# PSUM tiles of one bank from the beginning, and values and crosses of a double step taken pair of heads by pair of heads

## The chip, the core and the metric

The kernel runs on one core of one Trainium2 chip. The metric is the device time of one execution in microseconds. Three runs of the kernel before took 953.83, 954.51 and 955.61 us, so its median is 954.51 us. One further execution was profiled.

## The reference

A decayed linear attention (8 batches, 8 heads, 576 positions, head size 64) is followed by a feed-forward layer with a softplus, over all 4,608 tokens, in float32:

```python
scores = scale * np.matmul(q, k.transpose(0, 1, 3, 2))
Dmat = np.where(rel >= 0, gamma[:, None, None] ** rel[None, :, :], 0.0)
attn = np.matmul(scores * Dmat[None], v)                    # B, H, S, D
x = attn.transpose(0, 2, 1, 3).reshape(B * S, H * D)         # 4608 x 512
h = x @ w_in                                                 # 512 -> 2048
g = np.maximum(h, 0.0) + np.log1p(np.exp(-np.abs(h)))
out = g @ w_out                                              # 2048 -> 512
```

## The kernel before

**Attention.** The tokens are cut into 36 chunks of 128, and the heads into 4 pairs. The decays are moved into q, k and v by scale factors, so that a chunk of a pair of heads needs masked scores within the chunk, their product with v (the *values*), a product of q with a running state of 64 x 64 per head (the *crosses*), and a new state. A cross is left out in the first chunk of a batch, and where a batch starts at row 64 of a chunk it covers 64 columns.

The first 9 chunks are computed in plain float32, in 18 *double steps* `m` of two pairs of heads each (`s` is the pair, `h` the head in it). `scores_double` (L154) gives TensorE four score matmuls (L160, 64 rows of weights by 128 columns of weights) and four state matmuls (L165, weights of 128 rows by 64 columns). `scores_double_out` (L169) has VectorE read them out with the mask (L175) and read out the state (L184 or L186), and GpSimd decays the state (L188). `values_double` (L191) gives TensorE four value matmuls (L200, weights 128 rows by 64 columns) and then four crosses (L206, weights 64 rows by 64 columns), which add to what the value matmuls wrote. `values_double_out` (L210) has ScalarE (L215) and VectorE (L216) write the result as a high and a low part into the x tile. TensorE works a float32 matmul off in two passes, each with its own weight load, so every such matmul has two MATMUL rows in the trace. The other 27 chunks go one pair at a time through matmuls of rounded parts (L265, L274, L347); the change doesn't touch them.

**Feed-forward.** 9 units of 512 tokens times 16 pieces of the hidden layer give 144 *slots*. Slot `i` has 12 matmuls of 512 columns for the hidden piece (`hidden_mm`, L379), the logarithm and exponential on ScalarE (L387 to L389), the softplus and its split on VectorE and ScalarE (L393 to L398), and 12 matmuls of 512 columns for the output of the slot before (`output_mm`, L411).

**The order is written out by hand** and each engine works its instructions off in that order. The *opening* runs double steps 0 to 8 before the first slot, while inputs and the first weight pieces are still arriving: in turn `scores_double(m)` and `values_double(m - 1)`. Double step 8 ends in slot 0: its values come behind the 12 hidden matmuls. Then every odd slot begins with `scores_double` and every even one with `values_double`, for double steps 9 to 17, up to slot 18. All of this is on TensorE between the matmuls of the slots. SyncE issues the loads; a load into a buffer waits until that buffer has been read.

**PSUM** has 8 banks of 512 float32 columns. Before, the attention tiles hold two banks each. In the opening three of them (`ps_open`: two for the scores in turn, one for the values of every other step) lie in six banks on the right, and one (`ps_att`) in the two on the left. In front of slot 0 the pool on the right is closed, and its banks go to the hidden tiles (`ps_h`, two) and the output tiles (`ps_y`, four); their first users wait for the last readers of the closed pool. From slot 0 on, scores and values take the one tile on the left in turn, so `scores_double(9)` waits until L216 has read the values of step 8:

```python
idle = two_banks(3)                                        # L504
open_pools.close()                                         # L537
later["ps_h"] = ctx.enter_context(tc.tile_pool(name="ps_h", bufs=2, space=PSUM, side="right"))
scores_double(m, two_banks(2))                             # L549
```

Of the kernel before, what the change touches and what calls it, by code (L numbers as in the profile page):

```python
# [7 lines left out]
F32 = mybir.dt.float32  # L8
# [5 lines left out]
PSUM = bass.MemoryType.PSUM  # L14


B, H, S, D = 8, 8, 576, 64
DM, DF = 512, 2048
NTOK = B * S
P = 128  # L20
C = 128
# [3 lines left out]
T = 512  # L25
CPU = T // C
# [7 lines left out]
AHEAD = STEPS // 2 + 1  # L34
# [25 lines left out]
def retention_softplus_ffn(ctx: ExitStack, tc, opening, first, others, w, dec, vsc, gchp, out):  # L60
    nc = tc.nc
# [6 lines left out]

    nc.scalar.preload_act_table_set("natural_log_exp_and_others")


    open_pools, plain_pools, weight_pools = ExitStack(), ExitStack(), ExitStack()
    ps_open = open_pools.enter_context(tc.tile_pool(name="ps_open", bufs=1, space=PSUM, side="right"))
    ps_att = plain_pools.enter_context(tc.tile_pool(name="ps_att", bufs=1, space=PSUM))
    rawp = plain_pools.enter_context(tc.tile_pool(name="rawp", bufs=2))
    pconst = plain_pools.enter_context(tc.tile_pool(name="pconst", bufs=1))
    wst = weight_pools.enter_context(tc.tile_pool(name="wst", bufs=WBUFS, side="right"))
    later = {}
# [15 lines left out]
    live = {}  # L94
# [56 lines left out]
            for n in range(4):  # L151
                nc.scalar.activation(v[:, n], v[:, n], AF.Copy, scale=f[:, n:n + 1])

    def scores_double(m, bank):  # L154

        L = live[-1 - m]
        for s in range(2):
            for h in range(2):
                rows = slice(h * D, (h + 1) * D)
                nc.tensor.matmul(bank[:, h, s * C:(s + 1) * C], L["k"][rows, s], L["q"][rows, s], start=True, stop=True)  # L160
        if _chunk_kind(m // 2)[1]:
            for s in range(2):
                for h in range(2):
                    rows = slice(h * D, (h + 1) * D)
                    nc.tensor.matmul(bank[rows, 0, 2 * C + s * D:2 * C + (s + 1) * D], L["kp"][:, s, rows],  # L165
                                     L["v"][:, s, rows], start=True, stop=True, skip_group_check=True)
        L["bank"] = bank

    def scores_double_out(m):  # L169
        L = live[-1 - m]  # L170
        start, follows = _chunk_kind(m // 2)
        a = moe.tile([P, 2, 2, C], F32, tag="osb", name="a2")
        msk = mask2 if start else mask
        for h in range(2):
            nc.vector.tensor_mul(a[:, h], L["bank"][:, h, 0:2 * C].rearrange("p (s c) -> p s c", s=2),  # L175
                                 msk.unsqueeze(1).broadcast_to([P, 2, C]))
        L["a"] = a
        L["before"] = states.get(m % 2)
        states[m % 2] = None
        if follows:  # L180
            st = L["bank"][:, 0, 2 * C:3 * C].rearrange("p (s d) -> p s d", s=2)
            s = att.tile([P, 2, D], F32, tag="s", name="s2", bufs=NPAIR + 1)
            if start is None:
                nc.vector.tensor_add(s, st, L["before"])  # L184
            else:
                nc.vector.tensor_copy(s, st)  # L186
            half = m % 2
            nc.gpsimd.tensor_mul(s, s, gchp0_sb[:, 2 * half:2 * half + 2].unsqueeze(2).broadcast_to([P, 2, D]))  # L188
            states[m % 2] = s

    def values_double(m, bank):  # L191
        L = live[-1 - m]
        start, _ = _chunk_kind(m // 2)
        n_cross = C if start is None else start
        if L["before"] is None:
            n_cross = 0
        for s in range(2):
            for h in range(2):
                rows = slice(h * D, (h + 1) * D)
                nc.tensor.matmul(bank[rows, s, 0:C], L["v"][:, s, rows], L["a"][:, h, s], start=True,  # L200
                                 stop=not n_cross, skip_group_check=True)
        if n_cross:
            for s in range(2):
                for h in range(2):
                    rows = slice(h * D, (h + 1) * D)
                    nc.tensor.matmul(bank[rows, s, 0:n_cross], L["before"][rows, s], L["q"][rows, s, 0:n_cross],  # L206
                                     start=False, stop=True, skip_group_check=True)
        L["o"] = bank

    def values_double_out(m):  # L210
        o = live.pop(-1 - m)["o"][:, :, 0:C]
        ch, pr = m // 2, 2 * (m % 2)
        xt = x_tile(ch // CPU)
        cols = slice((ch % CPU) * C, (ch % CPU + 1) * C)
        nc.scalar.copy(xt[:, HI, pr:pr + 2, cols], o)  # L215
        nc.vector.tensor_sub(xt[:, LO, pr:pr + 2, cols], o, xt[:, HI, pr:pr + 2, cols].bitcast(F32))  # L216
# [152 lines left out]
    ys = {}  # L369

    def hidden_mm(i, cols=slice(0, T)):

        u, p = divmod(i, NF)
        xt = x_tile(u)
        h = later["ps_h"].tile([P, T], F32, tag="h", name="h")[:, cols]
        n = 0
        for a, b in TERMS:
            for kt in range(NKT):
                nc.tensor.matmul(h, ws[p][:, a, kt * P:(kt + 1) * P], xt[:, b, kt, cols],  # L379
                                 start=(n == 0), stop=(n == 3 * NKT - 1))  # L380
                n += 1
        return h
# [18 lines left out]
    def output_mm(i):  # L401
        u, p = divmod(i, NF)
        parts = gs.pop(i)
        if p == 0:
            ys[u] = [later["ps_y"].tile([P, DM], F32, tag=f"y{n}", name=f"y{n}") for n in range(CPU)]
        for tt in range(CPU):
            y = ys[u][tt]
            for n, (a, b) in enumerate(TERMS):
                g = parts[tt * len(parts) // CPU]
                at = tt % (CPU // len(parts)) * P  # L410
                nc.tensor.matmul(y, g[:, a, at:at + P], ws[p][:, b, PIECE:],  # L411
                                 start=(p == 0 and n == 0), stop=(p == NF - 1 and n == 2))
# [83 lines left out]
            load_double(next_double[0])  # L496
            next_double[0] += 1

    def two_banks(n):
        pool, tag = ((ps_open, "open0"), (ps_open, "open1"), (ps_att, "bank"), (ps_open, "open2"))[n]  # L500
        return pool.tile([P, 2, 4 * C], F32, tag=tag, name="bank")


    idle = two_banks(3)  # L504
    for n in range(OPENING):
        nc.tensor.matmul(idle[:, n % 2, 0:2 * C], fill[:, 0:P], fill[:, 0:2 * C], start=True, stop=True)
    scale_next()
    scale_next()
    scale_values(0)
    for m in range(AHEAD):  # L510
        if m < AHEAD - 1:
            scores_double(m, two_banks(m % 2))
        if m > 0:
            values_double(m - 1, two_banks(2 + m % 2))
        if m == AHEAD - 1:
            scores_double(m, two_banks(m % 2))
            values_double_out(m - 1)
        if m in (2, 3, 4, 7, 8):
            load_next()
        if m in (3, 5, 7):  # L520
            load_weight((m + 1) // 2)
        scale_values(m + 1)
        scores_double_out(m)
        if m in (2, 4, 7):
            weight_b(m // 2 - 1)
        if m in (3, 5):
            weight_d((m - 3) // 2)
        if 0 < m < AHEAD - 1:
            values_double_out(m - 1)
        if m in (2, 4, 7):  # L530
            weight_c(m // 2 - 1)
        if m in (1, 3, 6):
            weight_a(m // 3)
        scale_next()
    weight_d(START_WEIGHTS - 1)
    wpos[0] = START_WEIGHTS
    open_pools.close()  # L537
    later["ps_h"] = ctx.enter_context(tc.tile_pool(name="ps_h", bufs=2, space=PSUM, side="right"))
    later["ps_y"] = ctx.enter_context(tc.tile_pool(name="ps_y", bufs=1, space=PSUM, side="right"))


    SPLIT = NPLAIN - LEAD
    deferred = [lambda: None]
    for i in range(NSLOT):
        j = i + LEAD
        if i < SPLIT:
            m = AHEAD + (i - 1) // 2
            if i % 2:
                scores_double(m, two_banks(2))  # L549
                scores_double_out(m)  # L550
                scale_next()
                if "raw" in later:
                    load_upto(NPLAIN + 1)
            elif i:
                values_double(m, two_banks(2))
                values_double_out(m)
                load_next()
            weight_step()
# [16 lines left out]
                scale_step(j + 2)  # L575
        else:
            scores_mm(j)
            bank = later["ps_os"].tile([P, 4 * C], F32, tag="os", name="os")
            value_mm(j - 1, bank)
            state_mm(j, bank)  # L580
            scale_step(j + 2)
            rest = value_out(j - 1)
            scores_out(j)
# [7 lines left out]
            break  # L591
        h = hidden_mm(i)
        if i == 0:
            values_double(AHEAD - 1, two_banks(2))
        ab = logs(h)
        if i == 0:
            values_double_out(AHEAD - 1)
# [85 lines left out]
```

## Time and profile before

| | |
|---|---|
| median of three runs | 954.51 us (953.83 to 955.61) |
| time of the profiled execution | 954.67 us |
| its span, first to last instruction | 952.9 us |
| TensorE matmul busy | 942.0 us, 99% of the span |
| ScalarE, VectorE, GpSimd busy | 676.9, 665.2 and 279.7 us |
| mean granted TensorE clock | 1.000 of full speed |

The profiled execution lasts 1.8 us longer than its span, and 0.16 us longer than the median of the runs. The chain of waits names, going back from the last instruction, what each step waited for; it shows where time can be won or lost. Rows of a timeline give the start of a group, the time from its first start to its last end, and, in brackets, how long the engine stood idle before it. Matmuls are pipelined, so such a group reaches into the next one: how long it holds TensorE is the distance from its start to the start of the next group.

### The profile page before, as it was taken

Reading aid. Unit: us, or ns where it says so; the run is one execution under the profiler, and the core shown is the slowest. Engines: PE = TensorE matmul, PEld = TensorE weight load, DVE = VectorE, ACT = ScalarE, POOL = GpSimd, SP = SyncE. Lnnn points to the kernel's source line nnn. Section 1 sums busy time; section 2 is a strip of 40 time slices with the busy share of each in tenths; the row PEclk is TensorE's granted clock in tenths of the full one; section 3 lists DMA queues with packets and bytes.
Section 4 is the critical chain, followed back from the end, with each engine's and each line's share of the span. In section 5 each row is a group of like instructions: output and inputs, shape, how many; then the busy total and the mean of one; then the engine's idle time right before and its main releaser. Section 6 shows DMA issues by size and latency. Waiting matters only on the chain.

```text
span 952.9 us, 14502 instructions
## 1 busy us (share of the span) xinstructions
PE 942.0 (99%) x4946; PEld 789.4 (83%) x4946; DVE 665.2 (70%) x1507; ACT 676.9 (71%) x1449; POOL 279.7 (29%) x497
## 2 busy tenths in 40 slices
PE   8899999999999999999999999999999999999998
PEld 6677778888888888888888888888888888888886
DVE  6688855777877777777777777777777777753222
ACT  6677756777877777777777777777777777764444
POOL 5122103333342332333343333233333333310000
PEclk9999999999999999999999999999999999999999
DMA  8556623212312132212212132213212222201001
GB/s 299 199 171 205 199 82 112 59 58 67 98 63 67 52 109 67 64 53 94 80 55 67 58 104 67 67 51 111 67 50 67 67 95 67 67 1 45 1 1 44
DMA packets 28729, 79.85 MB, mean 84 GB/s; under 512 B 3440, under 2 KB 3440, under 8 KB 28656
## 3 DMA queue, kind: packets, MB, share of 16 engines
q1 hardware_dynamic: 28656, 78.93, 26.1%
q8 instruction: 39, 0.64, 0.3%
q14 instruction: 34, 0.28, 0.1%
HBM read 69.48 MB, written 9.44 MB: 83 GB/s over the span
## 4 chain that ended last, share of the span: by engine, by line
PE 96%; DMA 2%; SPq 0%; POOL 0%; issue 0%; ACT 0%; POOLq 0%
PE h L379 42%; PE y L411 41%; PE os L347 6%; PE sc L265 3%; PE os L274 2%; DMA raw_g<-first 1%; PE bank L160 1%; PE bank L200 1%; PE bank L206 1%; DMA raw_rawp<-first 1%; PE bank L165 0%; SPq L437 0%; SPq L120 0%; POOL raw_g L136 0%; SPq L110 0%
## 5 line engine op out<-in xcount | busy, mean ns | idle before, releaser
L379 PE MATMUL h<-xt,w 128*128 128x512 f32 (+1 forms) x1740 | 420.6, 390 | 1.3 <-DVE s L186 1.3
L411 PE MATMUL y<-w,g 128*128 128x512 f32 x1728 | 414.9, 389 | 0.0
L411 PEld LDWEIGHTS y<-w,g 128*128 128x128 f32 x1728 | 324.3, 188 | 67.2
L379 PEld LDWEIGHTS h<-xt,w 128*128 128x128 f32 x1740 | 316.8, 188 | 63.5 <-ACT wst L443 1.4
L240 POOL TENSOR_TENSOR raw<-raw,dec_sb 128x256 f32<-128x256 f32 x108 | 98.3, 910 | 436.7 <-DMA raw<-others 404.6
L398 DVE TENSOR_TENSOR g<-ab,g 128x512 fp32r<-128x512 f32 (+1 forms) x145 | 101.3, 699 | 96.6 <-ACT g L397 96.6
L397 ACT CAST g<-ab 128x512 fp32r<-128x512 f32 (+1 forms) x145 | 89.5, 617 | 109.0 <-DVE ab L393 107.8
L393 DVE SCALAR_TENSOR_TENSOR ab<-h,ab 128x512 f32<-128x512 f32 (+1 forms) x145 | 99.6, 687 | 84.8 <-ACT ab L389 82.2
L387 ACT ACTIVATE ab<-h 128x512 f32<-128x512 f32 (+1 forms) x145 | 86.3, 595 | 76.6 <-PE h L379 76.4
L389 ACT ACTIVATE ab<-ab 128x512 f32<-128x512 f32 (+1 forms) x145 | 91.3, 630 | 4.6
L388 ACT ACTIVATE ab<-ab 128x512 f32<-128x512 f32 (+1 forms) x145 | 91.2, 629 | 4.6
L254 ACT CAST hl<-raw 128x768 fp32r<-128x768 f32 x108 | 91.0, 842 | 0.7 <-POOL raw L245 0.7
L284 DVE TENSOR_TENSOR a<-sc,a 128x256 f32<-128x256 f32 x108 | 45.8, 424 | 61.9 <-ACT a L283 61.6
L360 ACT CAST xt<-os 64x128 fp32r<-64x128 f32 x216 | 56.3, 261 | 44.3 <-PE os L274 40.1
L256 DVE TENSOR_TENSOR hl<-raw,hl 128x512 fp32r<-128x512 f32 x108 | 85.2, 789 | 1.5
L347 PE MATMUL os<-ah,hl 128*128 128x256 f32 x324 | 72.7, 285 | 0.0
L364 DVE TENSOR_TENSOR xt<-os,xt 64x128 fp32r<-64x128 f32 x216 | 62.3, 288 | 2.8
L308 POOL TENSOR_TENSOR s<-s,gchp_sb 128x128 f32<-128x128 f32 x96 | 59.4, 619 | 10.6 <-DVE s L307 0.2
L347 PEld LDWEIGHTS os<-ah,hl 128*128 128x128 f32 x324 | 53.3, 191 | 0.1
L285 POOL TENSOR_SCALAR_AFFINE_SELECT a<-a 128x256 f32<-128x256 f32 x108 | 44.2, 409 | 28.4 <-DVE a L284 26.7
L255 DVE TENSOR_TENSOR hl<-raw,hl 64x256 fp32r<-64x256 f32 x108 | 45.9, 425 | 7.6 <-ACT hl L254 4.6
L316 ACT CAST ah<-a 128x256 fp32r<-128x256 f32 x108 | 44.0, 407 | 7.6 <-POOL a L285 4.6
(84 smaller groups left out, 784.9 us busy)
## 6 DMA issues: line engine op xcount, KB each, us to landing
raw<-others SPq DMA_DIRECT2D x108, 384.0 KB, 3.1
wst<-w SPq DMA_DIRECT2D x32, 512.0 KB, 3.9
out<-osb SPq DMA_DIRECT2D x34, 256.0 KB, 2.2
raw_rawp<-first SPq DMA_DIRECT2D x13, 512.0 KB, 4.6
raw_g<-first SPq DMA_DIRECT2D x3, 512.0 KB, 7.5
raw_ab<-first SPq DMA_DIRECT2D x2, 256.0 KB, 8.6
dec_sb<-dec SPq DMA_DIRECT2D x1, 512.0 KB, 3.8
out<-part SPq DMA_DIRECT2D x2, 256.0 KB, 2.8
```

Source lines behind the costliest of these rows:

```text
L240: nc.gpsimd.tensor_mul(r[:, 2:4], r[:, 2:4], later["dec"][:, 2 * pr:2 * pr + 2])
L254: nc.scalar.copy(hl[:, 0:6], r)
L256: nc.vector.tensor_sub(hl[:, 6:10], r[:, 2:6], hl[:, 2:6].bitcast(F32))
L347: nc.tensor.matmul(o[:, :, 0:width], lhs, rhs, start=(n == 0), stop=(n == len(mms) - 1))
L379: nc.tensor.matmul(h, ws[p][:, a, kt * P:(kt + 1) * P], xt[:, b, kt, cols], start=(n == 0), stop=(n == 3 * NKT - 1))
L387: nc.scalar.activation(ab, h, AF.Abs)
L388: nc.scalar.activation(ab, ab, AF.Exp, scale=-1.0)
L389: nc.scalar.activation(ab, ab, AF.Ln, bias=1.0)
L393: nc.vector.scalar_tensor_tensor(ab, h, 0.0, ab, op0=ALU.max, op1=ALU.add)
L397: nc.scalar.copy(g[:, HI], ab)
L398: nc.vector.tensor_sub(g[:, LO], ab, g[:, HI].bitcast(F32))
L411: nc.tensor.matmul(y, g[:, a, at:at + P], ws[p][:, b, PIECE:], start=(p == 0 and n == 0), stop=(p == NF - 1 and n == 2))
```

## The change

All PSUM tiles have one bank, and the pools of the later stage are there from the beginning: `ps_y` (four banks) and `ps_h` (two) on the right, `ps_att` with two single banks on the left. The scores of a double step of the opening take two of the output banks in turn (y0 and y1, or y2 and y3), its values one of the two banks on the left. No pool is closed before slot 0. From slot 0 on the scores take both banks on the left, one for each head, and the values one. The values of both pairs of heads stand now in the right half of one bank, and the matmuls that write them are taken in another order: values and crosses of the first pair of heads, then values and crosses of the second.

```diff
-    open_pools, plain_pools, weight_pools = ExitStack(), ExitStack(), ExitStack()
-    ps_open = open_pools.enter_context(tc.tile_pool(name="ps_open", bufs=1, space=PSUM, side="right"))
-    ps_att = plain_pools.enter_context(tc.tile_pool(name="ps_att", bufs=1, space=PSUM))
+    ps_y = ctx.enter_context(tc.tile_pool(name="ps_y", bufs=1, space=PSUM, side="right"))
+    ps_h = ctx.enter_context(tc.tile_pool(name="ps_h", bufs=2, space=PSUM, side="right"))
+    plain_pools, weight_pools = ExitStack(), ExitStack()
+    ps_att = plain_pools.enter_context(tc.tile_pool(name="ps_att", bufs=2, space=PSUM))
...
-    def scores_double(m, bank):
+    def scores_double(m, banks):
...
-                nc.tensor.matmul(bank[:, h, s * C:(s + 1) * C], L["k"][rows, s], L["q"][rows, s], start=True, stop=True)
+                nc.tensor.matmul(banks[h][:, s * C:(s + 1) * C], L["k"][rows, s], L["q"][rows, s], start=True, stop=True)
...
+        o = bank[:, 2 * C:4 * C].rearrange("p (s c) -> p s c", s=2)
         for s in range(2):
             for h in range(2):
                 rows = slice(h * D, (h + 1) * D)
-                nc.tensor.matmul(bank[rows, s, 0:C], L["v"][:, s, rows], L["a"][:, h, s], start=True,
+                nc.tensor.matmul(o[rows, s], L["v"][:, s, rows], L["a"][:, h, s], start=True,
                                  stop=not n_cross, skip_group_check=True)
-        if n_cross:
-            for s in range(2):
-                for h in range(2):
-                    rows = slice(h * D, (h + 1) * D)
-                    nc.tensor.matmul(bank[rows, s, 0:n_cross], L["before"][rows, s], L["q"][rows, s, 0:n_cross],
-                                     start=False, stop=True, skip_group_check=True)
-        L["o"] = bank
+            for h in range(2) if n_cross else ():
+                rows = slice(h * D, (h + 1) * D)
+                nc.tensor.matmul(o[rows, s, 0:n_cross], L["before"][rows, s], L["q"][rows, s, 0:n_cross],
+                                 start=False, stop=True, skip_group_check=True)
+        L["o"] = o
...
-    idle = two_banks(3)
+    def bank():
+        return ps_att.tile([P, 4 * C], F32, tag="bank", name="bank")
+    idle = ps_h.tile([P, T], F32, tag="h", name="idle")
...
     for m in range(AHEAD):
+        pair = [ps_y.tile([P, 4 * C], F32, tag=f"y{2 * (m % 2) + h}", name="pair") for h in range(2)]
         if m < AHEAD - 1:
-            scores_double(m, two_banks(m % 2))
+            scores_double(m, pair)
         if m > 0:
-            values_double(m - 1, two_banks(2 + m % 2))
+            values_double(m - 1, bank())
...
-    open_pools.close()
-    later["ps_h"] = ctx.enter_context(tc.tile_pool(name="ps_h", bufs=2, space=PSUM, side="right"))
-    later["ps_y"] = ctx.enter_context(tc.tile_pool(name="ps_y", bufs=1, space=PSUM, side="right"))
...
-                scores_double(m, two_banks(2))
+                scores_double(m, [bank() for _ in range(2)])
...
-                values_double(m, two_banks(2))
+                values_double(m, bank())
```

On VectorE, ScalarE, GpSimd and SyncE the instructions stand in the same order as before; only TensorE's order differs. In the rows below `a_...` is the masked scores, `s_...` the state, `raw_...` a loaded input of a double step, `h` and `y` the hidden and output tiles, `w_...` and `xt_...` the weights and the x tile.

TensorE at the end of the opening (double steps 6, 7 and 8), before:

```order
L200 MATMUL bank<-a_356,raw_rawp 64x128 x4
L206 MATMUL bank<-raw_rawp,s_292 64x128 x4
L200 MATMUL bank<-a_394,raw_rawp 64x128 x4
L206 MATMUL bank<-raw_rawp,s_327 64x128 x4
L160 MATMUL bank<-raw_g 128x128 x4
L165 MATMUL bank<-raw_g 64x64 x4
L379 MATMUL h<-xt_190,w_94 128x512 x12
```

and now, where L203, L207, L162, L167 and L380 are the lines that were L200, L206, L160, L165 and L379:

```order
L203 MATMUL bank<-a_366,raw_rawp 64x128 x2
L207 MATMUL bank<-raw_rawp,s_300 64x128 x2
L203 MATMUL bank<-a_366,raw_rawp 64x128 x2
L207 MATMUL bank<-raw_rawp,s_300 64x128 x2
L203 MATMUL bank<-a_405,raw_rawp 64x128 x2
L207 MATMUL bank<-raw_rawp,s_336 64x128 x2
L203 MATMUL bank<-a_405,raw_rawp 64x128 x2
L207 MATMUL bank<-raw_rawp,s_336 64x128 x2
L162 MATMUL pair<-raw_g 128x128 x4
L167 MATMUL pair<-raw_g 64x64 x4
L380 MATMUL h<-xt_195,w_97 128x512 x12
```

Groups of four have become groups of two, and values and crosses alternate twice as often; nothing else has moved.

TensorE in front of and behind the hidden matmuls of slot 0, with the semaphores that an instruction waits for, before:

```order
L379 MATMUL h<-xt_190,w_94 128x512 [waits DVE_49,PE_49,Activation_49]
L379 MATMUL h<-xt_190,w_94 128x512
L379 MATMUL h<-xt_190,w_94 128x512 [waits Activation_49]
L379 MATMUL h<-xt_190,w_94 128x512 x9
L200 MATMUL bank<-a_429,raw_g 64x128 x4
L206 MATMUL bank<-raw_g,s_359 64x64 x4
L160 MATMUL bank<-raw_rawp 128x128 [waits DMAHW7_49,DVE_49,Pool_49]
L160 MATMUL bank<-raw_rawp 128x128 x3
```

and now (from the seventh hidden matmul on, with the five behind it):

```order
L380 MATMUL h<-xt_195,w_97 128x512 [waits DVE_49]
L380 MATMUL h<-xt_195,w_97 128x512 x5
L203 MATMUL bank<-a_441,raw_g 64x128 [waits DVE_49] x2
L207 MATMUL bank<-raw_g,s_369 64x64 x2
L203 MATMUL bank<-a_441,raw_g 64x128 x2
L207 MATMUL bank<-raw_g,s_369 64x64 x2
L162 MATMUL bank<-raw_rawp 128x128 [waits DMAHW7_49,PE_49,Pool_49]
L162 MATMUL bank<-raw_rawp 128x128 [waits DVE_49]
L162 MATMUL bank<-raw_rawp 128x128 x2
```

The first hidden matmul no longer waits for VectorE: that wait stands now at the fifth and seventh, which read the low part of the x tile. The wait for VectorE in front of the scores of step 9 has gone from their first matmul to their second, which writes the bank of the values of step 8.

TensorE at the front of an even slot, before:

```order
L411 MATMUL y_543<-w_96,g 128x512 x3
L200 MATMUL bank<-a_625,raw_rawp 64x128 x4
L206 MATMUL bank<-raw_rawp,s_432 64x128 x4
L379 MATMUL h<-xt_190,w_98 128x512 x12
L411 MATMUL y_540<-w_97,g 128x512 x3
```

and now:

```order
L412 MATMUL y_549<-w_99,g 128x512 x3
L203 MATMUL bank<-a_632,raw_rawp 64x128 x2
L207 MATMUL bank<-raw_rawp,s_444 64x128 x2
L203 MATMUL bank<-a_632,raw_rawp 64x128 x2
L207 MATMUL bank<-raw_rawp,s_444 64x128 x2
L380 MATMUL h<-xt_195,w_101 128x512 x12
```

Between the 512-column matmuls stand the same eight small ones, with three changes between L203 and L207 where there was one.

## Rows read from the trace of the kernel before

**Rows 1.** Chain of waits that ended last, share of the span by line.

```profile
PE h L379 42%; PE y L411 41%; PE os L347 6%; PE sc L265 3%; PE os L274 2%; DMA raw_g<-first 1%; PE bank L160 1%; PE bank L200 1%; PE bank L206 1%; DMA raw_rawp<-first 1%; PE bank L165 0%; SPq L437 0%; SPq L120 0%; POOL raw_g L136 0%; SPq L110 0%
```

**Rows 2.** Busy time by stretch: the span's microseconds, their sum, then each engine.

```profile
32.00:152.00 120.00, 120.00 (x701) 93.43 (x702) 87.99 (x159) 82.63 (x141) 20.11 (x25) 1.00 0.51 165
```

**Rows 3.** Timeline of TensorE, 17.9 to 26.3 us: start, extent, engine, line, shapes, count.

```profile
18.50 0.71 PE L160 MATMUL bank<-raw_rawp 64*128 64x128 f32 x8 [0.80 <-POOL raw_rawp L136]
19.14 0.45 PE L165 MATMUL bank<-raw_rawp 128*64 128x64 f32 x8
19.42 0.61 PE L200 MATMUL bank<-a,raw_ab 128*64 128x128 f32 x8
19.96 0.65 PE L206 MATMUL bank<-raw_ab,s 64*64 64x128 f32 x8
...
22.01 0.65 PE L206 MATMUL bank<-raw_rawp,s 64*64 64x128 f32 x8
22.59 0.66 PE L200 MATMUL bank<-a,raw_rawp 128*64 128x128 f32 x8
23.18 0.65 PE L206 MATMUL bank<-raw_rawp,s 64*64 64x128 f32 x8
23.77 0.72 PE L160 MATMUL bank<-raw_g 64*128 64x128 f32 x8
24.41 0.45 PE L165 MATMUL bank<-raw_g 128*64 128x64 f32 x8
26.18 0.47 PE L379 MATMUL h<-xt,w 128*128 128x512 f32 x1 [1.31 <-DVE s L186]
```

**Rows 4.** Timeline of TensorE, 28.9 to 33.1 us.

```profile
29.07 0.66 PE L200 MATMUL bank<-a,raw_g 128*64 128x128 f32 x8
29.66 0.45 PE L206 MATMUL bank<-raw_g,s 64*64 64x64 f32 x8
31.96 0.72 PE L160 MATMUL bank<-raw_rawp 64*128 64x128 f32 x8 [1.86 <-issue]
32.61 0.45 PE L165 MATMUL bank<-raw_rawp 128*64 128x64 f32 x8
32.99 0.50 PE L379 MATMUL h<-xt,w 128*128 128x512 f32 x1
```

**Rows 5.** Timeline of TensorE, 38.7 to 39.7 us.

```profile
39.24 0.45 PE L206 MATMUL bank<-raw_rawp,s 64*64 64x64 f32 x8
39.62 0.50 PE L379 MATMUL h<-xt,w 128*128 128x512 f32 x1
```

**Rows 6.** Timeline of TensorE, 52.0 to 53.2 us.

```profile
52.02 0.66 PE L200 MATMUL bank<-a,raw_rawp 128*64 128x128 f32 x8
52.60 0.65 PE L206 MATMUL bank<-raw_rawp,s 64*64 64x128 f32 x8
53.19 0.50 PE L379 MATMUL h<-xt,w 128*128 128x512 f32 x1
```

**Rows 7.** Groups of TensorE by line and shape, 31.9 to 160 us: busy, mean ns.

```profile
L206 PE MATMUL bank<-raw_rawp,s 64*64 64x128 f32 x64 | 5.2, 282 | 0.0
...
L206 PE MATMUL bank<-raw_rawp,s 64*64 64x64 f32 x8 | 0.4, 230 | 0.0
```

**Rows 8.** Timelines of ScalarE, VectorE and GpSimd, 24.3 to 31.9 us.

```profile
24.35 0.36 ACT L215 CAST xt<-bank 128x256 fp32r<-128x256 f32 x1
...
29.23 0.60 ACT L387 ACTIVATE ab<-h 128x512 f32<-128x512 f32 x1 [3.94 <-PE h L379]
...
31.05 0.35 ACT L215 CAST xt<-bank 128x256 fp32r<-128x256 f32 x1
...
25.75 0.28 DVE L186 COPY s<-bank 128x128 f32<-128x128 f32 x1
...
31.44 0.42 DVE L216 TENSOR_TENSOR xt<-bank,xt 128x256 fp32r<-128x256 f32 x1 [3.32 <-ACT xt L215]
...
27.77 0.81 POOL L142 TENSOR_TENSOR raw_rawp<-raw_rawp,part 128x256 f32<-128x256 f32 x1
```

More of the change, by code (lines that the diff above doesn't have):

```diff
@@ L164, in scores_double @@
                     rows = slice(h * D, (h + 1) * D)
-                    nc.tensor.matmul(bank[rows, 0, 2 * C + s * D:2 * C + (s + 1) * D], L["kp"][:, s, rows],
+                    nc.tensor.matmul(banks[0][rows, 2 * C + s * D:2 * C + (s + 1) * D], L["kp"][:, s, rows],
                                      L["v"][:, s, rows], start=True, stop=True, skip_group_check=True)
-        L["bank"] = bank
+        L["banks"] = banks
     def scores_double_out(m):
@@ L174, in scores_double_out @@
         for h in range(2):
-            nc.vector.tensor_mul(a[:, h], L["bank"][:, h, 0:2 * C].rearrange("p (s c) -> p s c", s=2),
+            nc.vector.tensor_mul(a[:, h], L["banks"][h][:, 0:2 * C].rearrange("p (s c) -> p s c", s=2),
                                  msk.unsqueeze(1).broadcast_to([P, 2, C]))
@@ L180, in scores_double_out @@
         if follows:
-            st = L["bank"][:, 0, 2 * C:3 * C].rearrange("p (s d) -> p s d", s=2)
+            st = L["banks"][0][:, 2 * C:3 * C].rearrange("p (s d) -> p s d", s=2)
             s = att.tile([P, 2, D], F32, tag="s", name="s2", bufs=NPAIR + 1)
@@ L199, in values_double @@
                 rows = slice(h * D, (h + 1) * D)
-                nc.tensor.matmul(bank[rows, s, 0:C], L["v"][:, s, rows], L["a"][:, h, s], start=True,
+                nc.tensor.matmul(o[rows, s], L["v"][:, s, rows], L["a"][:, h, s], start=True,
                                  stop=not n_cross, skip_group_check=True)
-        if n_cross:
-            for s in range(2):
-                for h in range(2):
-                    rows = slice(h * D, (h + 1) * D)
-                    nc.tensor.matmul(bank[rows, s, 0:n_cross], L["before"][rows, s], L["q"][rows, s, 0:n_cross],
-                                     start=False, stop=True, skip_group_check=True)
-        L["o"] = bank
+            for h in range(2) if n_cross else ():
[3 more added lines that the diff above has]
+        L["o"] = o
     def values_double_out(m):
-        o = live.pop(-1 - m)["o"][:, :, 0:C]
+        o = live.pop(-1 - m)["o"]
         ch, pr = m // 2, 2 * (m % 2)
@@ L374, in hidden_mm @@
         xt = x_tile(u)
-        h = later["ps_h"].tile([P, T], F32, tag="h", name="h")[:, cols]
+        h = ps_h.tile([P, T], F32, tag="h", name="h")[:, cols]
         n = 0
@@ L404, in output_mm @@
         if p == 0:
-            ys[u] = [later["ps_y"].tile([P, DM], F32, tag=f"y{n}", name=f"y{n}") for n in range(CPU)]
+            ys[u] = [ps_y.tile([P, DM], F32, tag=f"y{n}", name=f"y{n}") for n in range(CPU)]
         for tt in range(CPU):
@@ L497, in load_next @@
             next_double[0] += 1
-    def two_banks(n):
-        pool, tag = ((ps_open, "open0"), (ps_open, "open1"), (ps_att, "bank"), (ps_open, "open2"))[n]
-        return pool.tile([P, 2, 4 * C], F32, tag=tag, name="bank")
-    idle = two_banks(3)
+    def bank():
+        return ps_att.tile([P, 4 * C], F32, tag="bank", name="bank")
+    idle = ps_h.tile([P, T], F32, tag="h", name="idle")
     for n in range(OPENING):
-        nc.tensor.matmul(idle[:, n % 2, 0:2 * C], fill[:, 0:P], fill[:, 0:2 * C], start=True, stop=True)
+        nc.tensor.matmul(idle[:, 0:2 * C], fill[:, 0:P], fill[:, 0:2 * C], start=True, stop=True)
     scale_next()
@@ L510, in retention_softplus_ffn @@
     for m in range(AHEAD):
+        pair = [ps_y.tile([P, 4 * C], F32, tag=f"y{2 * (m % 2) + h}", name="pair") for h in range(2)]
         if m < AHEAD - 1:
-            scores_double(m, two_banks(m % 2))
+            scores_double(m, pair)
         if m > 0:
-            values_double(m - 1, two_banks(2 + m % 2))
+            values_double(m - 1, bank())
         if m == AHEAD - 1:
-            scores_double(m, two_banks(m % 2))
+            scores_double(m, pair)
             values_double_out(m - 1)
@@ L536, in retention_softplus_ffn @@
     wpos[0] = START_WEIGHTS
-    open_pools.close()
-    later["ps_h"] = ctx.enter_context(tc.tile_pool(name="ps_h", bufs=2, space=PSUM, side="right"))
-    later["ps_y"] = ctx.enter_context(tc.tile_pool(name="ps_y", bufs=1, space=PSUM, side="right"))
     SPLIT = NPLAIN - LEAD
-    deferred = [lambda: None]
     for i in range(NSLOT):
@@ L577, in retention_softplus_ffn @@
             scores_mm(j)
-            bank = later["ps_os"].tile([P, 4 * C], F32, tag="os", name="os")
-            value_mm(j - 1, bank)
-            state_mm(j, bank)
+            os = later["ps_os"].tile([P, 4 * C], F32, tag="os", name="os")
+            value_mm(j - 1, os)
+            state_mm(j, os)
             scale_step(j + 2)
@@ L593, in retention_softplus_ffn @@
         if i == 0:
-            values_double(AHEAD - 1, two_banks(2))
+            values_double(AHEAD - 1, bank())
         ab = logs(h)
```

## The prediction

> **What bounds the kernel now.** I read the chain of waits first. Of the span, 83% are the hidden and output matmuls, and nearly all that is left is TensorE too [rows 1]. The table by stretches says the same for the part in which double steps stand between the slots: from 32 to 152 us TensorE is busy for 120.00 of 120.00 us [rows 2]. Whatever is added to TensorE there is added to the end, and VectorE and ScalarE, with some 88 and 83 us, are never last. In the opening TensorE does wait, so I read its timeline there. Three waits matter: 0.80 us in front of the scores of step 6, for an input that GpSimd has to scale [rows 3]; 1.31 us in front of the hidden matmuls of slot 0, for VectorE's copy L186 of the state of step 8 [rows 3]; and 1.86 us in front of the scores of step 9 [rows 4].
>
> The last one is put down to "issue", so I looked for what ended there. GpSimd was done with the input of step 9 at 27.77 + 0.81 = 28.58 us. VectorE's L216, which reads the values of step 8 out of the tile that the scores need, ended at 31.44 + 0.42 = 31.86, and the scores began at 31.96 [rows 4, 8]. L216 it is. It comes late because ScalarE takes the logarithm of slot 0 (from 29.23) before its own read L215 (31.05) [rows 8]. So everything behind 31.96 hangs on when the hidden matmuls of slot 0 end.
>
> **The changed order on TensorE, in the slots.** The number of matmuls, their shapes and columns stay. What changes is how often neighbours differ in shape: values use the array as 128*64, crosses as 64*64. Before, a double step has two such changes (values to crosses, crosses to what follows) besides the one on entry; now it has four. The price of one change can be read in two parts:
> - Leaving: L165 followed by L200 of the same shape holds TensorE for 19.42 - 19.14 = 0.28 us [rows 3]; followed by the 128*128 hidden matmuls, 32.99 - 32.61 = 0.38 us [rows 4]. So 0.10 us.
> - Entering: L200 behind L165 of the same shape takes 19.96 - 19.42 = 0.54 us, behind crosses 23.18 - 22.59 = 0.59 us [rows 3]. So 0.05 us.
>
> Together 0.15 us. Both directions that are added stand in the trace: 52.02 to 52.60 values, 52.60 to 53.19 crosses [rows 6], and crosses followed by values, 22.01 to 22.59, hold 0.58 us just like crosses followed by anything else [rows 3]. With crosses of 64 columns the group holds 0.38 us [rows 5]; the 0.21 us less are four passes of half as many columns, and the price of the change is still in it. So a double step grows from 0.59 + 0.59 = 1.18 to about 1.48 us, by 2 x 0.15 = 0.30 us.
>
> From 31.9 us on there are 72 rows of L206, eight for a double step, so 9 double steps [rows 7]. Their addition is 9 x 0.30 = **2.70 us**, with nothing to hide it.
>
> The trace shows no group of two, only of four. Bounds from the nearest rows: nothing, if TensorE gets ready for the next shape while the last group drains, and at the other end what the scores pay. Their group holds 24.41 - 23.77 = 0.64 us [rows 3]; a pass of 128 columns costs 2 x 0.21 / 4 = 0.10 us by the comparison above, four of them 0.41, which leaves 0.23 us for entering and leaving. That gives 0 to 18 x 0.23 = 4.1 us. I take 0.15, because it is read from these shapes themselves.
>
> The Trainium skill has a rule that speaks against this change: in "TensorEngine Tiling (Array Packing)", section "Key Properties", it says that changing the tiling mode (not just the tile) drains the TensorE, and gives no figure. The trace agrees with its 0.10 us on leaving; the 0.05 us on entering go beyond the rule.
>
> **The opening.** Two things pull in opposite directions. The wait for L186 falls away: the hidden tile no longer comes from a closed pool, and the first hidden matmul needs ScalarE's L215 alone. Against it, the six steps 2 to 7 have crosses and grow by 0.30 us each. For steps 2 to 4 that is 0.90 us against the 0.80 us in which TensorE waits for GpSimd in front of step 6, so about 0.1 us comes through. Steps 5 to 7 then add 0.90 us with no wait in between [rows 3]. The scores of step 8 end 1.0 us later. Without a wait the hidden matmuls follow them at 24.41 + 0.38 = 24.79 us; with 1.0 us on top at 25.79, in place of 26.18 [rows 3]: **0.39 us earlier**. L215 of step 7 moves with the values of step 7 and ends near 24.71 + 1.0 = 25.7 [rows 8], in time for the third matmul, which is the one to need it.
>
> From there the 0.39 us runs on: hidden matmuls end, L387 starts near 28.84, L215 at 30.66, L216 ends at 31.47, and the scores of step 9 go on at about 31.57. Splitting the scores into two banks lets their first matmul go ahead, but the second writes the bank that L216 reads, so the wait stays and all but a few hundredths of it count. Nothing else becomes last: the load of step 9 waits for the values of step 6 and starts some 0.7 us later, so GpSimd ends near 29.3 instead of 28.58; the values of step 8 end near 28.68 + 1.27 = 29.95, before ScalarE wants them at 30.66. The loads of weights and of step 10 that stand behind it in SyncE's queue move by up to 1 us and are first used behind 33 us. Bounds: at best the full wait is won, 26.18 - 24.79 = 1.39 us; at worst the hidden matmuls still wait for VectorE, whose work on step 8 comes 1.0 us later, and 1.0 us is lost.
>
> The filler matmuls at the start go to one bank instead of two; they run before the first input is scaled. Reads by VectorE and ScalarE keep their sizes. Both are costed at nothing.
>
> **Sum.** -0.39 + 2.70 = +2.31 us on the profiled 954.67 us is 956.98; that execution lies 0.16 us above the median of the runs, so 956.8 us.
>
> **Rivals.**
> 1. Only the draining is paid, 0.10 us a change, because with two matmuls a group the next weights are loaded meanwhile. For it: the drain is the larger part. Against it: the entering price is there in every group of rows 3 to 6. The slots then add 1.80 us; in the opening steps 2 to 4 vanish in the wait, steps 5 to 7 add 0.60, the hidden matmuls start at 25.39, 0.79 us earlier. Together +1.0: 955.5 us.
> 2. Not slower: the changes cost nothing, as TensorE works the two heads' parts of the array off side by side and lets one shape run into the other. Then only the freed wait counts: -1.39, so 953.1 us. It decides from the price of a change downward at which 18 in the slots and 6 in the opening equal 1.39 us, 0.058 us. Against it: 0.15 us at every change in the rows.
> 3. A change is as dear as the scores', 0.23 us. Slots +4.1; opening 1.38 - 0.80 = 0.58 through the wait and 1.38 behind it, so 24.79 + 1.96 = 26.75 us, +0.57. Together +4.7: 959.2 us. For it: groups of two might pair worse than groups of four. Against it: shapes and directions are those of the cheaper rows.
> 4. The change doesn't do what it says in the opening: the hidden matmuls still end up behind VectorE, by the low part of the x tile. Then +1.0 + 2.70: 958.2 us. Against it: the fifth matmul is the first to wait for VectorE, some 1 us in.
>
> **How the numbers follow.** Forecast 0.64, own range 956.1 to 957.5; rival 1 0.13, rival 2 0.06, rival 3 0.07, rival 4 0.10. The range 955.2 to 958.4 takes in rivals 1 and 4 and leaves out 0.13. A difference under 0.2%, 1.9 us, is about what a measurement of this kernel can't tell from none. The forecast of +2.3 stands only 0.4 above that; I give a quarter of it, 0.16, to "within", with rival 1 and half of rival 2: 0.32. Faster is the other half of rival 2, 0.03, and slower the rest, 0.65.
>
> **What the profile after would show.** In the slots, an even slot with a cross of 128 columns: L203 to the hidden matmuls 1.47 us rather than 1.17, four groups of four rows, about 0.37 us each. The hidden matmuls of slot 0 at about 25.8 us with little idle in front, the scores of step 9 running on near 31.6, TensorE without a gap behind that. If the four groups take 1.2 us together, the step on the changes of shape is wrong; if the hidden matmuls begin at 26.2 or later, the step on the opening; if TensorE stands idle behind 32 us, the bound is.

## The result, and the profile after

| | before | changed |
|---|---|---|
| median, runs of one comparison (17 each) | 955.61 us (953.83 to 957.24) | 957.75 us (956.72 to 961.78) |
| ratio | | 1.003, 95% interval 1.0022 to 1.0038 |
| profiled execution, span | 954.67 and 952.9 us | 961.63 and 959.8 us |
| mean granted clock of the profiled execution | 1.000 | 0.995 |

The changed kernel is slower by 0.3%: some 2.9 us by the ratio, 2.14 us between the medians, where 2.3 us were forecast. Its median lies inside the forecast range, 0.95 us above the forecast, but 7 of its 17 executions lie above the range. And the kernel before itself came out 1.1 us above the 954.51 us on which that time was built.

The profiled execution of the changed kernel is among its slowest, and it can't be laid beside the one of before as it is: its TensorE fell twice to the lower of its two clock levels, 1.2 of 2.4 GHz. The table by stretches shows where. Its columns are those of [rows 2]: the stretch, its length, the busy time of TensorE's matmuls, TensorE's weight loads, VectorE, ScalarE and GpSimd, then the granted clock, and the share and GB/s of the DMA.

```profile
4.00:8.00 4.00, 2.61 (x22) 1.81 (x20) 0.95 (x3) 1.06 (x4) 0.67 (x1) 1.00 0.94 335
8.00:12.00 4.00, 3.05 (x28) 2.50 (x30) 0.95 (x3) 2.43 (x10) 1.91 (x4) 0.53 1.02 413
12.00:16.00 4.00, 4.00 (x46) 3.15 (x46) 3.27 (x8) 2.87 (x10) 2.46 (x4) 0.61 0.66 231
...
36.00:40.00 4.00, 4.00 (x12) 3.14 (x13) 3.89 (x9) 2.32 (x4) 0.51 (x1) 0.63 0.30 71
```

The mean clock is 0.53 from 8 to 12 us, 0.61 from 12 to 16 and 0.63 from 36 to 40. The timeline of TensorE in the same execution (start, extent, idle before) has a wait in front of each fall:

```profile
8.95 1.22 PE L162 MATMUL pair<-raw_rawp 64*128 64x128 f32 x8 [2.34 <-POOL raw_rawp L138]
...
34.68 0.71 PE L162 MATMUL bank<-raw_rawp 64*128 64x128 f32 x6 [1.11 <-DVE xt L217]
...
35.75 4.52 PE L380 MATMUL h<-xt,w 128*128 128x512 f32 x12
40.11 2.91 PE L412 MATMUL y<-w,g 128*128 128x512 f32 x12
...
44.21 3.02 PE L380 MATMUL h<-xt,w 128*128 128x512 f32 x12
47.06 0.62 PE L412 MATMUL y<-w,g 128*128 128x512 f32 x2
```

TensorE stood idle for 2.34 us for the input of step 1, which GpSimd scales, and for 1.11 us for VectorE. Twelve hidden matmuls of slot 1 then held it for 40.11 - 35.75 = 4.36 us; in the next slot it was 47.06 - 44.21 = 2.85. The wait for the input is longer than in the profile of before, though ahead of it only the bank of the filler matmuls was changed. There it was 0.31 us:

```profile
7.70 0.72 PE L160 MATMUL bank<-raw_rawp 64*128 64x128 f32 x8 [0.31 <-POOL raw_rawp L136]
```

It differs from execution to execution: the scores of step 1 begin at 8.95 us here, and at 7.56 in another execution of the same kernel.

That execution (the first experiment below) was profiled at full clock: 956.84 us, span 955.1. It is the one to lay beside [rows 3 and 4], the timeline of TensorE in the opening:

```profile
7.56 0.71 PE L162 MATMUL pair<-raw_rawp 64*128 64x128 f32 x8
...
18.47 0.71 PE L162 MATMUL pair<-raw_rawp 64*128 64x128 f32 x8
...
24.63 0.71 PE L162 MATMUL pair<-raw_g 64*128 64x128 f32 x8
25.28 0.45 PE L167 MATMUL pair<-raw_g 128*64 128x64 f32 x8
25.66 3.02 PE L380 MATMUL h<-xt,w 128*128 128x512 f32 x12
...
29.87 0.49 PE L162 MATMUL bank<-raw_rawp 64*128 64x128 f32 x2
31.47 0.71 PE L162 MATMUL bank<-raw_rawp 64*128 64x128 f32 x6 [1.11 <-DVE xt L217]
...
32.49 3.06 PE L380 MATMUL h<-xt,w 128*128 128x512 f32 x12
35.38 2.88 PE L412 MATMUL y<-w,g 128*128 128x512 f32 x12
```

The hidden matmuls follow the step in front of them without idle time, at 25.66 us where it was 26.18. The first score matmul of step 9 (two rows) goes ahead, the other three wait, and the row names VectorE's read now. They go on at 31.47 in place of 31.96. The output matmuls begin at 35.38; in the execution with the two falls it was 40.11, 4.73 us later, and that is all of the 4.7 us between the two spans. ScalarE and VectorE in that stretch of the same execution:

```profile
28.77 0.60 ACT L388 ACTIVATE ab<-h 128x512 f32<-128x512 f32 x1 [3.08 <-PE h L380]
...
30.60 0.35 ACT L216 CAST xt<-bank 128x256 fp32r<-128x256 f32 x1
...
30.99 0.42 DVE L217 TENSOR_TENSOR xt<-bank,xt 128x256 fp32r<-128x256 f32 x1 [2.16 <-ACT xt L216]
```

They answer to [rows 8]: the read ends at 31.41, and the scores go on 0.06 us later. In the slots, the double step that answers to [rows 6]:

```profile
51.83 0.44 PE L203 MATMUL bank<-a,raw_rawp 128*64 128x128 f32 x4
52.20 0.43 PE L207 MATMUL bank<-raw_rawp,s 64*64 64x128 f32 x4
52.57 0.44 PE L203 MATMUL bank<-a,raw_rawp 128*64 128x128 f32 x4
52.94 0.43 PE L207 MATMUL bank<-raw_rawp,s 64*64 64x128 f32 x4
53.30 3.01 PE L380 MATMUL h<-xt,w 128*128 128x512 f32 x12
```

Four groups at 0.37 us hold TensorE for 1.47 us, where two held it for 1.17. From where the scores of step 9 go on to the end of the span are 955.1 - 31.47 = 923.63 us; before, it was 952.9 - 31.96 = 920.94 [rows 4]. The difference is 2.69 us, and TensorE still has no gap in the table by stretches (as [rows 2]):

```profile
32.00:152.00 120.00, 120.00 (x685) 90.86 (x684) 86.47 (x159) 81.91 (x138) 19.70 (x24) 1.00 0.52 165
```

### The profile page after: what moved, and what is told of

It is laid out like the page before. It is cut to its first block, busy times and chain, and to the rows that moved or that the text cites. A ratio compares the mean times of both kernels' runs of the same rounds, so it can differ in the third digit from the quotient of the medians.

```text
span 959.8 us, 14501 instructions
## 1 busy us (share of the span) xinstructions
PE 950.4 (99%) x4946; PEld 792.0 (83%) x4946; DVE 665.3 (69%) x1507; ACT 678.3 (71%) x1449; POOL 284.4 (30%) x497
## 4 chain that ended last, share of the span: by engine, by line
PE 98%; DMA 1%; ACT 0%; SPq 0%; POOL 0%; issue 0%; DVE 0%; ACTq 0%; POOLq 0%
PE h L380 42%; PE y L412 41%; PE os L348 6%; PE sc L266 3%; PE os L275 2%; PE bank L203 1%; PE bank L207 1%; PE pair L162 1%; DMA raw_rawp<-first 1%; PE bank L162 1%; PE pair L167 0%; PE bank L167 0%; SPq L112 0%; POOL raw_rawp L138 0%; ACT ab L389 0%; ACT ab L390 0%
## 5 line engine op out<-in xcount | busy, mean ns | idle before, releaser
L380 PE MATMUL h<-xt,w 128*128 128x512 f32 (+1 forms) x1740 | 422.0, 391 | 0.0
L380 PEld LDWEIGHTS h<-xt,w 128*128 128x128 f32 x1740 | 317.9, 189 | 62.6 <-issue 1.4
L241 POOL TENSOR_TENSOR raw<-raw,dec_sb 128x256 f32<-128x256 f32 x108 | 102.5, 949 | 433.9 <-DMA raw<-others 409.5
```

Of the source, the lines that this page charges most:

```text
L241: nc.gpsimd.tensor_mul(r[:, 2:4], r[:, 2:4], later["dec"][:, 2 * pr:2 * pr + 2])
```

## The experiments

Theory 1 is that the changes of shape cost 2.7 us in the slots, of which the opening gives back a little. Its rival, theory 2, is that the layout in single banks costs and the order does not. A second question is the clock. In what follows, full clock is a mean granted clock of 0.999 or 1.000 over an execution.

**The changed kernel again.** No edit.

> The changed kernel once more, for more runs of it beside the kernel before and, where TensorE keeps its full clock, a profile at that clock. Theory 1 (the changes of shape cost 0.15 us each, 2.7 us in the slots, and the opening gives back 0.4 us; what lies above that is half clock in some executions): about +2.3 us against before where the mean clock is 1.000, and 1 to 4 us more where it is below. Theory 2 (the layout of the banks costs, not the order): the same total, but without groups of 0.37 us. In a profile at full clock theory 1 wants the hidden matmuls of slot 0 near 25.8 us and the scores of step 9 running on near 31.6.

Measured: 958.06 us (956.77 to 958.74) against 955.23, ratio 1.0026 (1.0014 to 1.0038). Its profile is the one above: 25.66 where 25.8 was expected, 31.47 where 31.6 was, groups of 0.37 us. Theory 1 holds. Two of the six executions were at full clock (956.77 and 956.84), four at 0.997 (958.06 to 958.74). The two lie 2.26 us above the median of the ten executions of the kernel before that were at full clock in the same comparison (954.55); about 2.3 was expected.

**One bank, grouped order.** The tiles of the changed kernel, the order of the one before:

```diff
-                nc.tensor.matmul(o[rows, s], L["v"][:, s, rows], L["a"][:, h, s], start=True,
+                nc.tensor.matmul(o[rows, s], L["v"][:, s, rows], L["a"][:, h, s], start=(s == 0),
                                  stop=not n_cross, skip_group_check=True)
-            for h in range(2) if n_cross else ():
-                ...
+        if n_cross:
+            for s in range(2):
+                for h in range(2):
+                    rows = slice(h * D, (h + 1) * D)
+                    nc.tensor.matmul(o[rows, s, 0:n_cross], L["before"][rows, s], ...
```

> One-bank tiles as in the changed kernel, but all four values of a double step and then its four crosses, as before (the values of the second pair don't open an accumulation group of their own, so that the first pair's sum in the same bank is kept). Theory 1: the 2.7 us in the slots go, and the wait of 1.31 us in front of slot 0 is gone without anything in its place: 1.3 us faster than before, ratio about 0.9986. Theory 2: as slow as the changed kernel, ratio about 1.003.

Measured: 953.70 us (952.21 to 956.47) against 955.23, ratio 0.9987 (0.9978 to 0.9997). Its timeline of TensorE:

```profile
22.67 0.75 PE L203 MATMUL bank<-a,raw_rawp 128*64 128x128 f32 x8
...
24.15 0.72 PE L162 MATMUL pair<-raw_g 64*128 64x128 f32 x8
...
25.18 3.02 PE L382 MATMUL h<-xt,w 128*128 128x512 f32 x12
...
30.98 0.71 PE L162 MATMUL bank<-raw_rawp 64*128 64x128 f32 x6 [1.41 <-DVE xt L219]
...
34.86 2.88 PE L414 MATMUL y<-w,g 128*128 128x512 f32 x12
37.67 0.66 PE L203 MATMUL bank<-a,raw_rawp 128*64 128x128 f32 x8
...
51.03 0.66 PE L203 MATMUL bank<-a,raw_rawp 128*64 128x128 f32 x8
51.62 0.65 PE L209 MATMUL bank<-raw_rawp,s 64*64 64x128 f32 x8
52.20 0.97 PE L382 MATMUL h<-xt,w 128*128 128x512 f32 x3
```

The double step holds TensorE for 52.20 - 51.03 = 1.17 us as before, and the hidden matmuls follow the scores without a wait. The layout alone wins 1.0 us in the profiles (scores going on at 30.98 in place of 31.96, span 951.9 in place of 952.9), where 1.3 was expected. The 0.3 us are lost just ahead of slot 0: from the values of step 7 to the scores of step 8 it is 24.15 - 22.67 = 1.48 us here and 23.77 - 22.59 = 1.18 before [rows 3]. Theory 2 is out.

**The kernel before, interleaved order.** Two-bank tiles and the closed pool stay:

```diff
                 nc.tensor.matmul(bank[rows, s, 0:C], L["v"][:, s, rows], L["a"][:, h, s], start=True,
                                  stop=not n_cross, skip_group_check=True)
-        if n_cross:
-            for s in range(2):
-                for h in range(2):
-                    ...
+            for h in range(2) if n_cross else ():
+                rows = slice(h * D, (h + 1) * D)
+                nc.tensor.matmul(bank[rows, s, 0:n_cross], L["before"][rows, s], ...
```

> The kernel before with its two-bank tiles and its pool that is closed in front of slot 0; only values and crosses are taken pair of heads by pair of heads. Theory 1: 9 x 0.30 = 2.7 us in the slots, and in the opening about 1.0 us, since the wait for L186 stays and comes later: 3 to 4 us slower than before, ratio 1.003 to 1.004. Theory 2: no change, ratio 1.000.

Measured: 959.52 us (958.07 to 960.83) against 955.23, ratio 1.0043 (1.003 to 1.0056). Its timeline of TensorE:

```profile
28.02 3.01 PE L377 MATMUL h<-xt,w 128*128 128x512 f32 x12 [1.17 <-DVE s L186]
...
33.85 0.71 PE L160 MATMUL bank<-raw_rawp 64*128 64x128 f32 x8 [1.56 <-issue]
...
34.87 4.61 PE L377 MATMUL h<-xt,w 128*128 128x512 f32 x12
39.32 2.90 PE L409 MATMUL y<-w,g 128*128 128x512 f32 x12
...
55.79 0.44 PE L200 MATMUL bank<-a,raw_rawp 128*64 128x128 f32 x4
56.16 0.43 PE L204 MATMUL bank<-raw_rawp,s 64*64 64x128 f32 x4
56.53 0.44 PE L200 MATMUL bank<-a,raw_rawp 128*64 128x128 f32 x4
```

The same groups of 0.37 us, and the wait for L186 still there, later than before. The order alone makes the kernel slower, by 0.43% or 4.1 us; the layout takes about a quarter of that back. This profile has a mean clock of 0.998, and TensorE falls where the changed kernel fell for the second time: behind the wait of 1.56 us in front of step 9, twelve hidden matmuls hold TensorE for 39.32 - 34.87 = 4.45 us. The stretch by itself:

```profile
36.00:40.00 4.00, 4.00 (x14) 3.19 (x13) 3.90 (x9) 1.88 (x4) 0.51 (x1) 0.71 0.48 127
```

**The changed kernel with fillers** in its two waits (`fillers(n)` is the loop of the opening's filler matmuls, made a function):

```diff
+        if m == 1:
+            fillers(3)
         if m < AHEAD - 1:
             scores_double(m, pair)
...
+            if i == 1:
+                for n in range(6):
+                    nc.tensor.matmul(idle[:, 0:C], mask, mask, start=True, stop=True)
             if i % 2:
                 scores_double(m, [bank() for _ in range(2)])
```

> The changed kernel with filler matmuls in its two long waits of the opening: three of 256 columns in front of the scores of step 1 and six of 128 columns in front of the scores of step 9. Theory on the clock (it falls because TensorE stands idle in these waits): mean clock 1.000 in all or nearly all runs, and a median as the quicker runs of the changed kernel, about 2.3 us above before. Rival (the falls have nothing to do with these waits): mean clock below 1.000 in about half of the runs, as with the changed kernel (8 of 17), and a median some 0.5 to 1 us higher than without the fillers.

Measured: 957.95 us (956.90 to 958.34) against 955.23, ratio 1.0027 (1.0018 to 1.0037). All nine executions were at full clock, against 11 of the 23 of the changed kernel without fillers, so the falls do hang on these waits. Which of the two matters is not told apart here, as both were filled. The expectation on the time failed: the median is that of the changed kernel, not of its quicker executions. The timeline of TensorE shows why:

```profile
7.55 1.56 PE L507 MATMUL idle<-fill 128*128 128x256 f32 x6
9.04 0.71 PE L162 MATMUL pair<-raw_rawp 64*128 64x128 f32 x8
...
27.15 3.02 PE L380 MATMUL h<-xt,w 128*128 128x512 f32 x12
...
31.36 1.60 PE L552 MATMUL idle<-mask 128*128 128x128 f32 x12
32.90 0.77 PE L162 MATMUL bank<-raw_rawp 64*128 64x128 f32 x8
```

The first fillers run from 7.55 to 9.04, where the full-clock execution without them began these scores at 7.56 us. The hidden matmuls come at 27.15 rather than 25.66, and the fillers use up what they save.

**A free bank for the scores of step 9.** The grouped kernel, with one statement changed:

```diff
-                scores_double(m, [bank() for _ in range(2)])
+                scores_double(m, [ps_y.tile([P, 4 * C], F32, tag="y3", name="pair") if i == h == 1 else bank()
+                                  for h in range(2)])
```

> The one-bank tiles with grouped values and crosses, and the scores of step 9 take the free bank on the left for the first head and the output bank y3, not yet in use then, for the second: they no longer wait for VectorE to read the values of step 8. Theory (the wait of 1.4 to 1.9 us in front of these scores is bound by that read alone): the scores run through near 29.3 us, the hidden matmuls of slot 1 begin near 30.3 instead of 32.0, the output matmuls follow near 33.3, and y3 waits 0.1 to 0.2 us for VectorE's mask. Some 1.6 us faster than the grouped kernel, 2.8 to 3 us faster than before, ratio about 0.997. With that wait gone the mean clock is below 1.000 less often. Rival (VectorE and ScalarE are the next to be late, by the split of slot 0 or the weights of slot 1): the wait only moves in front of the output matmuls, and the time is that of the grouped kernel, ratio 0.9985.

Measured: 952.87 us (951.45 to 954.45) against 956.12, ratio 0.9967 (0.9957 to 0.9976), faster than the kernel before and than the changed one. Three of eleven executions are below full clock, against 13 of 17 of the kernel before in the same comparison. At full clock the median is 952.51 us, 1.0 us below the 953.53 of the grouped kernel (in another comparison), where 1.6 was expected. Its timeline of TensorE:

```profile
30.33 0.45 PE L167 MATMUL bank<-raw_rawp 128*64 128x64 f32 x8
30.72 3.03 PE L382 MATMUL h<-xt,w 128*128 128x512 f32 x12
33.71 3.34 PE L414 MATMUL y<-w,g 128*128 128x512 f32 x12
36.98 0.66 PE L203 MATMUL bank<-a,raw_rawp 128*64 128x128 f32 x8
```

The wait in front of the scores is gone. Part of it comes back where it was expected, but larger: the output matmuls of slot 0 hold TensorE for 36.98 - 33.71 = 3.27 us, in the grouped kernel for 37.67 - 34.86 = 2.81. That is 0.46 us, not 0.1 to 0.2. VectorE's mask, which reads y3, ends only at 35.55 + 0.42 = 35.97 us.

This profile also has a wait of 2.35 us in front of the scores of step 1, as long as the 2.34 in front of the first fall above, and no fall behind it. The row, and the stretch in the table:

```profile
8.74 0.72 PE L162 MATMUL pair<-raw_rawp 64*128 64x128 f32 x8 [2.35 <-POOL raw_rawp L138]
```

```profile
8.00:12.00 4.00, 3.00 (x48) 2.35 (x48) 2.09 (x7) 3.23 (x12) 2.42 (x5) 1.00 1.01 412
```

**The same with two fillers** in front of the scores of step 1.

```diff
+        if m == 1:
+            for n in range(2):
+                nc.tensor.matmul(idle[:, 0:2 * C], fill[:, 0:P], fill[:, 0:2 * C], start=True, stop=True)
```

> The same, with two filler matmuls of 256 columns in front of the scores of step 1. Theory on the clock: mean clock 1.000 or 0.999 in all runs; the median is 0.3 to 0.5 us below that of the kernel without them if half of its runs lose 1.3 us, less what the fillers (0.86 us) delay where the input is early. Rival: the fillers delay the opening by 0.5 us in each run, and the median is not below.

Measured: 952.69 us (951.37 to 953.04), ratio 0.9964 (0.9952 to 0.9975). All seven executions are at full clock. The median is 0.18 us below that without fillers, too little to tell the two expectations apart.

**The kernel before with fillers** in the same two waits (in front of step 9 into the bank of y3, not yet in use).

```diff
+        if m == 1:
+            for n in range(3):
+                nc.tensor.matmul(idle[:, n % 2, 0:2 * C], fill[:, 0:P], fill[:, 0:2 * C], start=True, stop=True)
...
+            if i == 1:
+                spare = later["ps_y"].tile([P, DM], F32, tag="y3", name="spare")
+                for n in range(6):
+                    nc.tensor.matmul(spare[:, 0:C], mask, mask, start=True, stop=True)
```

> The kernel before with the same filler matmuls as in the changed one: three of 256 columns in front of the scores of step 1, six of 128 columns in front of the scores of step 9. The forecast was set on 954.5 us for the kernel before; with the clock beside each execution, 14 of 37 executions of it have a mean clock of 1.000 and a median of 954.8 us, and 23 are below with a median of 956.1. Theory (the falls come from the waits of the opening, which the kernel before has as well): mean clock 1.000 or 0.999 in all runs, spread under 2 us, and a median of 954.8 plus up to 0.9 us for what the fillers delay. Rival (the falls are of the chip and have nothing to do with these waits): below 0.999 in about half of the runs, as without the fillers, and a median of 956 us or more.

Measured: 954.86 us (954.12 to 957.11) against 955.50, ratio 0.9995 (0.9987 to 1.0004). Eleven of twelve executions are at full clock, one has 0.998 (957.11 us), so the spread is 3.0 us and not under 2; of the kernel before in the same comparison 5 of 16 are. The median is where the theory wanted it. Its timeline of TensorE:

```profile
29.70 1.60 PE L554 MATMUL spare<-mask 128*128 128x128 f32 x12
31.63 0.71 PE L160 MATMUL bank<-raw_rawp 64*128 64x128 f32 x8 [0.33 <-issue]
```

The wait of 1.86 us [rows 4] is 0.33. The falls of the kernel before hang on these two waits, too; one of the twelve executions still has one.

## Why the prediction was right or wrong

**What bounds the kernel** was read rightly. TensorE has no gap from 32 to 852 us in either kernel (120.00 of 120.00 us, then 700.00 of 700.00), and all that was added there came out at the end.

**The price of a change of shape** was right: 1.47 us for the double step against 1.48 forecast, 2.69 us from the scores of step 9 to the end against 2.70. The price that was put together from two comparisons of neighbouring groups held for groups of two, which the trace of before did not contain. Rivals 1 (only the drain), 2 (nothing) and 3 (as dear as the scores') are out. Both halves of the change were then measured apart, 1.0043 for the order and 0.9987 for the layout.

**The opening** was nearly right for the two executions that were profiled at full clock. The hidden matmuls start 0.52 us earlier (0.39 forecast), and 0.49 us reach the scores of step 9, by the chain that was described: hidden matmuls, ScalarE's logarithm, its read, VectorE's read. The scores of step 6, which were to come 0.1 us late, began at 18.47 us and so not late at all. Rival 4 is out: no wait stands in front of the hidden matmuls. But the 0.80 us in which the 0.90 us of steps 2 to 4 were to vanish are a number of one execution. Where the order is grouped, the wait in front of step 6 is 0.20, 0.20, 0.20 and 0.21 us in the profiles of the four other kernels; with so little, some 0.7 us would come through instead of 0.1.

**The step that failed** is the last of the sum: "that execution lies 0.16 us above the median of the runs, so 956.8 us". It took one profiled execution at a mean clock of 1.000, and a median of three runs beside it, for what the kernel before does, and no term of the sum stands for the clock, in either kernel. The kernel before has its full clock in the smaller part of its executions:

| executions of all comparisons with their clock | mean clock 0.999 or 1.000 | below |
|---|---|---|
| kernel before | 19 of 53, median 954.45 us | 34, median 956.04 us |
| changed kernel | 11 of 23, median 957.17 us | 12, median 958.74 us |

So TensorE mostly falls to the lower level before, too, which costs 1.6 us between the medians. No such execution of the kernel before was profiled; that the falls are in the opening rests on the fillers, and on the profile of the same two-bank tiles with the interleaved order. Of the 34 executions, 28 have a mean clock of 0.998 and a median of 955.93 us, six 0.996 and 957.48: two steps of some 1.5 us from 954.45, as one fall and two would make, if each costs what the second one of the changed kernel did (4.36 - 2.85 = 1.5 us; an estimate).

The median of many runs lies between the two columns, at 955.2 to 956.1 in the four comparisons, and 956.8 is only some 1 us above it. Three runs are too few in the changed kernel as well: its first three took 961.63, 959.73 and 956.72 us, with clocks of 0.995, 0.997 and 1.000, and their median lies above the range.

The growth that was worked out, 2.3 us, was not far off. At full clock it is 2.17 us between the two profiled executions, 2.26 within the one comparison that has the clock of both kernels, and 2.72 in the left column of the table, where 9 of the 11 executions of the changed kernel are of a comparison without a clock for the kernel before. Whether the 0.4 us between 2.3 and 2.7 are real, and whether the shorter wait in front of step 6 makes them, is not shown. The falls are not seen to be more frequent with the change (12 of 23 against 34 of 53), so they lift both kernels. The forecast time was 0.95 us low because its base was 1.10 low, while the medians grew by 0.17 less than was forecast.

The profile of before could not have shown the falls, since it had none. But it had the wait of 1.86 us in front of step 9, one of the two that the fillers later filled (the other, in front of step 1, was only 0.31 us in it), and beside it stood runs from 953.83 to 955.61 us, a spread nearly as large as the forecast change. The text should have taken that spread as one of its terms instead of the 0.16 us.

## What to carry to other kernels

Where small matmuls of different array shapes stand between large ones, count how often the shape changes, and price a change from two groups in the trace that differ only in their neighbour. Here 18 changes at 0.15 us, with nothing to hide them, outweighed a freed wait of 1.31 us; layout and order could be had apart, and the better half alone, with a free bank for the one wait left, gave 0.9967. Before a forecast of a few tenths of a per cent, ask for the clock of several executions, not of the profiled one alone.

## What the runs showed of the hardware that was not expected

TensorE's clock fell after single waits in the opening, and not after each of them. In the profiled execution of the changed kernel TensorE had been idle for 2.34 us in front of the first fall and for 1.11 us in front of the second, and the stretch of 12 hidden matmuls behind the second held it 1.5 us longer. The same kernel with a wait of the same 1.11 us kept the full clock in another execution, and the kernel with the free bank kept it behind a wait of 2.35 us. The length of the wait alone does not decide, then; what does is not shown. Matmuls of no use in these waits held the clock at 0.999 or above in 27 of 28 executions of three kernels. Without them it was so in 30 of 76 executions of the kernel before and the changed one, and in 8 of 11 of the kernel with the free bank, where the wait in front of step 9 was gone already.
